# Moving four weight conversions of a dense MLP into the mixture-of-experts stage, and issuing a gather one expert earlier

## The chip, the cores and the metric

The kernel runs on one core of a Trainium2 chip. The metric is the device time of one execution in microseconds (us); the median of several runs is given. The core has TensorE (PE, matmuls; PEld is its loading of weights), VectorE (DVE), ScalarE (ACT), GpSimd (POOL) and SyncE (SP), which issues most of the transfers between the chip's main memory and the core's memory. Each engine works through its own list of instructions in order and waits on semaphores for the others.

## The reference, cut to what matters

Three blocks follow one another. Each takes the result of the one before.

```python
def _moe_ref(x, w_gate, w1, w2):              # x: the attention's output, 2304 tokens x 512
    logits = x @ w_gate
    expert_idx = np.argmax(logits, axis=1)
    ...
    for e in range(E):                        # 8 experts
        mask = expert_idx == e
        xe = x[mask]
        h = np.maximum(xe @ w1[e], 0.0)       # 512 -> 1024
        ye = h @ w2[e]                        # 1024 -> 512
        out[mask] = gate_w[mask, None] * ye
    return out.astype(np.float32)

def _moe2_ref(x, w_in, w_out):                # w_in and w_out are float64
    h = x @ w_in                              # 512 -> 2048
    g = np.where(pos, h, np.where(neg, 0.0, (h + beta) ** 2 / (4.0 * beta)))
    return (g @ w_out).astype(np.float32)     # 2048 -> 512
```

Ahead of them stands an attention with random features, which the change does not touch.

## The kernel before, in words

The attention is laid out by a planner (class Plan). From there on the order of every engine's instructions is the order in which the program is written.

Every product is made of three matmuls: each operand is split into a high part (rounded for the matmul) and a low part (the rest), and high x high, high x low and low x high are summed. So a weight chunk needs, after its load into a raw tile (wraw, three buffers), a high part wh on POOL (L270) and a low part wl. For w1 and w2 the low part is a subtraction on DVE (L279), which is put off to the next w_flush; for w_in and w_out it is a subtraction on POOL (L274). w_in and w_out are float64: before the split, each chunk of 128 x 512 numbers is turned into float32 by one ACT instruction (wx, L263) and three DVE instructions (wy L264, wy L265, wz L268).

The list wseq names all chunks in the order of their use: per expert four of w1 and four of w2, then per quarter of the dense MLP four of w_in and four of w_out. w_advance (L298) does one chunk: it flushes the low part of the chunk before, issues loads on SP up to two chunks beyond this one (w_fetch, ahead = 3) and starts the split. A load waits until the raw buffer that it takes over has been read, which for w1 and w2 means until the low part of the chunk three places before is done on DVE.

An expert e in the loop at L1097: eight hidden slices f = 0 to 7 (m_h): 12 matmuls (L984 to L986) into one of three PSUM buffers ph, then hh on ACT (L989) and hl on DVE (L990). After every even f one advance is made (a w2 chunk of this expert), after every odd f a flush. Then four output slices d = 0 to 3 (m_y, 24 matmuls each, L1002 to L1004, with yT copied out by ACT at L1007). Ahead of each, the tokens of the next expert are transposed (m_x, L946) and split into xh on ACT (L952) and xl on DVE (L953); the low part of the chunk before is flushed; after each one advance is made (a w1 chunk of the next expert). In experts 1 to 5 order_tokens adds three small DVE instructions (sob, sov) after odd f; in expert 5 it ends with a small store, ld (L1031), of 2304 single numbers to main memory.

The tokens of an expert are fetched by gather (L937): up to three indirect DMAs that POOL issues (L940), at the start of the expert before. At the start of the last expert stands overflow (L1037), a block of code behind a branch that is not taken with these inputs.

In the last expert the advances do its four w2 chunks, the first four chunks of w_in and three of w_out; z_split (L913) splits the columns of yT for the dense MLP into yh on ACT and yl on DVE (L919). The dense MLP (z_h, L1131) starts right behind.

## Time and profile before

| | |
|---|---|
| time, median of 3 runs | 843.32 us (840.59, 844.49, 843.32) |
| the profiled execution | 839.76 us, its span 838.0 us |
| mean granted clock of TensorE | 0.974 |
| PE busy | 783.4 us, 93% |
| PEld, DVE busy | 85%, 68% |
| ACT, POOL busy | 43%, 46% |

The span runs from the first to the last instruction. The attention ends near 170 us; the experts follow, each about 25 to 38 us long; the dense MLP's first matmuls stand near 420 us and the last matmul near 824 us. A busy share is an average over all these stages. Matmuls overlap, so that a matmul's own time is longer than the distance from one start to the next; a gap of PE is read from the idle time ahead of an instruction. The granted clock has two levels here, 1.0 (2.4 GHz) and 0.5 (1.2 GHz).

### The profile page before, as it was taken

Reading aid. Unit: us, or ns where it says so; the run is one execution under the profiler, and the core shown is the slowest. Engines: PE = TensorE matmul, PEld = TensorE weight load, DVE = VectorE, ACT = ScalarE, POOL = GpSimd, SP = SyncE. Lnnn points to the kernel's source line nnn. Section 1 sums busy time; section 2 is a strip of 40 time slices with the busy share of each in tenths; the row PEclk is TensorE's granted clock in tenths of the full one; section 3 lists DMA queues with packets and bytes.
Section 4 is the critical chain, followed back from the end, with each engine's and each line's share of the span. In section 5 each row is a group of like instructions: output and inputs, shape, how many; then the busy total and the mean of one; then the engine's idle time right before and its main releaser. Section 6 shows DMA issues by size and latency. Waiting matters only on the chain.

```text
span 838.0 us, 16906 instructions
## 1 busy us (share of the span) xinstructions
PE 783.4 (93%) x6530; PEld 714.3 (85%) x6530; DVE 573.9 (68%) x1122; ACT 357.7 (43%) x890; POOL 384.1 (46%) x387
## 2 busy tenths in 40 slices
PE   6898899689999999988899999999999999999994
PEld 5787788569999999988888989898989898989893
DVE  4789797955775576354988566686777877656631
ACT  6998799412222222211444554444343434343321
POOL 5547851544455434342565444454434543334343
PEclk9999899869999999999999999999999999999998
DMA  9876301255555545653522001110111100001111
GB/s 222 209 172 185 97 29 28 78 156 163 189 178 179 177 157 158 153 159 124 183 84 92 26 26 49 53 51 25 40 37 51 51 25 1 1 26 51 39 50 64
DMA packets 79036, 80.44 MB, mean 96 GB/s; under 512 B 28972, under 2 KB 61868, under 8 KB 78944
## 3 DMA queue, kind: packets, MB, share of 16 engines
q1 hardware_dynamic: 75056, 68.10, 28.4%
q0 software_dynamic: 3072, 9.57, 3.3%
q10 hardware_dynamic: 816, 1.57, 0.6%
q8 instruction: 54, 0.88, 0.4%
q14 instruction: 38, 0.31, 0.1%
HBM read 69.78 MB, written 9.45 MB: 95 GB/s over the span
## 4 chain that ended last, share of the span: by engine, by line
PE 48%; DVE 3%; DMA 2%; issue 1%; POOL 1%; ACT 0%; POOLq 0%; another core or an unknown queue 0%; DVEq 0%
PE po L1186 8%; PE po L1185 8%; PE po L1184 8%; PE ph L1140 8%; PE ph L1142 8%; PE ph L1141 8%; DVE wy L265 1%; DVE yl L919 1%; DMA out_dram<-acc,oidx 1%; DMA wraw<-in_moe_w_in_dram 1%; DMA wraw<-in_moe_w_dram 1%; DVE wy L264 0%; POOL gl L1169 0%; DVE wl L279 0%; PE ph L984 0%
## 5 line engine op out<-in xcount | busy, mean ns | idle before, releaser
L1169 POOL TENSOR_TENSOR gl<-cl,gh 128x384 fp32r<-128x384 f32 x96 | 104.6, 1110 | 167.5 <-ACT gh L1168 167.4
L1161 ACT ACTIVATE cl<-cl,half 128x384 f32<-128x384 f32 x96 | 57.0, 615 | 215.1 <-DVE cl L1160 215.1
L1141 PE MATMUL ph<-yl,wh 128*128 128x384 f32 x384 | 129.9, 338 | 1.8 <-DVE yl L919 1.8
L1140 PE MATMUL ph<-yh,wh 128*128 128x384 f32 x384 | 129.9, 338 | 0.0
L1142 PE MATMUL ph<-yh,wl 128*128 128x384 f32 x384 | 129.8, 338 | 0.0
L270 POOL TENSOR_SCALAR wh<-wraw 128x1024 fp32r<-128x1024 f32 x60 | 69.5, 1159 | 124.6 <-DMA wraw<-in_moe_w_dram 74.5
L1186 PE MATMUL po<-wh,gl 128*128 128x512 f32 x288 | 114.3, 397 | 0.1
L1185 PE MATMUL po<-wl,gh 128*128 128x512 f32 x288 | 113.8, 395 | 0.0
L1184 PE MATMUL po<-wh,gh 128*128 128x512 f32 x288 | 113.7, 395 | 0.0
L1160 DVE TENSOR_SCALAR cl<-ph 128x384 f32<-128x384 f32 x96 | 51.3, 550 | 77.8 <-PE ph L1142 77.0
L482 ACT ACTIVATE pp<-ps,bi 128x128 f32<-128x128 f32 x288 | 84.2, 476 | 6.1 <-DVE bi L478 6.1
L919 DVE TENSOR_TENSOR yl<-yT,yh 128x384 fp32r<-128x384 f32 x96 | 83.5, 927 | 4.3 <-ACT yh L918 4.3
L984 PE MATMUL ph<-xh,wh 128*128 128x288 f32 (+6 forms) x256 | 80.5, 314 | 5.8 <-DVE hl L990 3.2
L279 DVE TENSOR_TENSOR wl<-wraw,wh 128x1024 fp32r<-128x1024 f32 x60 | 75.0, 1251 | 12.1 <-POOL wh L270 12.1
L1002 PE MATMUL py<-hh,wh 128*128 128x288 f32 (+6 forms) x256 | 79.3, 310 | 1.8 <-ACT yT L1007 1.8
L985 PE MATMUL ph<-xl,wh 128*128 128x288 f32 (+6 forms) x256 | 78.8, 308 | 0.0
L986 PE MATMUL ph<-xh,wl 128*128 128x288 f32 (+6 forms) x256 | 78.6, 307 | 0.0
L1004 PE MATMUL py<-hh,wl 128*128 128x288 f32 (+6 forms) x256 | 76.8, 300 | 0.3 <-DVE wl L279 0.3
L1003 PE MATMUL py<-hl,wh 128*128 128x288 f32 (+6 forms) x256 | 76.5, 299 | 0.6 <-DVE hl L990 0.6
L1141 PEld LDWEIGHTS ph<-yl,wh 128*128 128x128 f32 x384 | 72.2, 188 | 4.1 <-DVE yl L919 2.2
L1140 PEld LDWEIGHTS ph<-yh,wh 128*128 128x128 f32 x384 | 72.2, 188 | 2.1
L1142 PEld LDWEIGHTS ph<-yh,wl 128*128 128x128 f32 x384 | 72.2, 188 | 0.0
(158 smaller groups left out, 1657.4 us busy)
## 6 DMA issues: line engine op xcount, KB each, us to landing
wraw<-in_moe_w_dram SPq DMA_DIRECT2D x57, 512.0 KB, 3.7
wraw<-in_moe_w_in_dram SPq DMA_DIRECT2D x16, 512.0 KB, 3.8
wraw<-in_moe_w_out_dram SPq DMA_DIRECT2D x16, 512.0 KB, 3.4
blk<-in_k_dram SPq DMA_DIRECT2D x8, 512.0 KB, 6.9
blk<-in_q_dram SPq DMA_DIRECT2D x8, 512.0 KB, 6.1
vm<-in_v_dram SPq DMA_DIRECT2D x16, 256.0 KB, 5.7
xd<-xr SPq DMA_DIRECT2D x16, 256.0 KB, 2.0
wra<-in_moe_w_dram SPq DMA_DIRECT2D x4, 512.0 KB, 7.1
```

What stands on the lines that cost most here:

```text
L482: act.activation(at(ppb)[:, 2 * j + i, :], at(pjb[i])[:, j, :], AF.Exp, bias=r["bi"][:, i, j:j + 1])
L919: nc.vector.tensor_sub(yl, yT[d][:, c], yh.bitcast(F32))
L984: nc.tensor.matmul(ph, lhsT=wh[:, d, c], rhs=xh, start=(d == 0), stop=False)
L985: nc.tensor.matmul(ph, lhsT=wh[:, d, c], rhs=xl, start=False, stop=False)
L1002: nc.tensor.matmul(py, lhsT=wh[:, a, c], rhs=hh, start=(f == 0), stop=False)
L1140: nc.tensor.matmul(ph[f], lhsT=wh[:, a, c], rhs=yh, start=(d == 0), stop=False)
L1141: nc.tensor.matmul(ph[f], lhsT=wh[:, a, c], rhs=yl, start=False, stop=False)
L1142: nc.tensor.matmul(ph[f], lhsT=wl[:, a, c], rhs=yh, start=False, stop=(d == 3))
L1169: nc.gpsimd.tensor_sub(gl, cl, gh.bitcast(F32))
L1184: nc.tensor.matmul(po, lhsT=gh[:, c], rhs=wh[:, a, :], start=(f == 0), stop=False)
L1185: nc.tensor.matmul(po, lhsT=gh[:, c], rhs=wl[:, a, :], start=False, stop=False)
L1186: nc.tensor.matmul(po, lhsT=gl[:, c], rhs=wh[:, a, :], start=False, stop=(f == 3))
```

## The change

A new kind of entry in wseq, ("early", chunk), stands behind the w2 chunks of experts 3, 4, 5 and 6, one for each of the four first w_in chunks. Its advance loads the float64 chunk and converts it (w_float32) into a float32 tile of its own, ws, of which there are four. Where the chunk has its old place in the last expert, nothing is loaded or converted any more; the high and low parts are taken from ws. The early advance is made at f = 6, straight behind that slice's own advance. The gather is issued in three parts after d = 1, 2 and 3, and for the expert after the next; expert 0 still issues the whole gather for expert 1 at its start.

```diff
     def w_load(key, t=None, dma=nc.sync):
-        kind, e, c = key
+        kind, e, c = key[1] if key[0] == "early" else key
...
+    def w_float32(t, out):
+
+        tv = t.rearrange("p (f two) -> p f two", two=2)
+        lv = tv[:, :, 0].bitcast(I32)
+        hv = tv[:, :, 1]
+        x = wp2[0].tile([P, 512], F32, name="wx", tag="wx", bufs=1)
+        y = wp2[0].tile([P, 512], I32, name="wy", tag="wy", bufs=1)
+        nc.scalar.activation(x, hv, AF.Copy, scale=2.0 ** -112)
+        nc.vector.tensor_scalar(out=y, in0=lv, scalar1=29, scalar2=None, op0=ALU.logical_shift_right)
+        nc.vector.scalar_tensor_tensor(out=y, in0=x.bitcast(I32), scalar=3, in1=y,
+                                       op0=ALU.logical_shift_left, op1=ALU.bitwise_or)
+        nc.vector.scalar_tensor_tensor(out=out.bitcast(I32), in0=hv.bitcast(I32), scalar=-2 ** 31, in1=y,
+                                       op0=ALU.bitwise_and, op1=ALU.bitwise_or)
...
     def w_split(key):
-        t = wraw.pop(key)
+        if key[0] == "early":
+
+            early = wearly[key[1]] = wst[0].tile([P, 512], F32, name="ws", tag="ws", bufs=4)
+            w_float32(wraw.pop(key), early)
+            return
+        t = wearly[key] if key in wearly else wraw.pop(key)
...
+            if key not in wearly:
+                raw, t = t, wp2[0].tile([P, 512], F32, name="wz", tag="wz", bufs=2)
+                w_float32(raw, t)
...
+    EARLY = {3 + c: ("wi", 0, c) for c in range(4)}
     for e in range(E):
         wseq += [("w1", e, c) for c in range(4)] + [("w2", e, c) for c in range(4)]
+        if e in EARLY:
+            wseq.append(("early", EARLY[e]))
...
         while wpos[0] < min(ahead[1], wpos[1] + ahead[0]):
-            w_load(wseq[wpos[0]], dma=dma)
+            if wseq[wpos[0]] not in EARLY.values():
+                w_load(wseq[wpos[0]], dma=dma)
             wpos[0] += 1
...
-        def gather(e):
-            t = mp.tile([P, NB, D], F32, name="xg", tag="xg", bufs=2)
+        def gather(e, parts=range(NB)):
+            if e >= E:
+                return
+            if 0 in parts:
+                xg[e] = mp.tile([P, NB, D], F32, name="xg", tag="xg", bufs=2)
             for i, r in rows(e):
-                nc.gpsimd.indirect_dma_start(
-                    out=t[0:r, i, :], out_offset=None, in_=xd,
-                    in_offset=bass.IndirectOffsetOnAxis(ap=gidx[0:r, i, e:e + 1], axis=0))
-            xg[e] = t
+                if i in parts:
+                    nc.gpsimd.indirect_dma_start(
+                        out=xg[e][0:r, i, :], out_offset=None, in_=xd,
+                        in_offset=bass.IndirectOffsetOnAxis(ap=gidx[0:r, i, e:e + 1], axis=0))
...
-            else:
-                gather(e + 1)
+            elif e == 0:
+                gather(1)
...
+                if f == 6 and e in EARLY:
+                    w_advance()
...
                     w_advance()
+
+                    if d:
+                        gather(e + 2, (d - 1,))
```

What this does to the lists of instructions is shown at three places, of the kernel before and then of the changed one. A row gives the line, the operation, what it writes and reads, and the shape. The line numbers of the changed kernel are others: L246, L247 and L249 are the three conversion instructions there, L288 is wl, L1010 hl, L973 xl, L279 wh, L961 the gather.

DVE in expert 4, from slice f = 5 to the first xl of expert 5, before:

```order
L279 TENSOR_TENSOR wl_3157<-wraw,wh_3156 128x1024
L990 SCALAR_TENSOR_TENSOR hl<-ph,hh 128x288 x2
L1014 TENSOR_SCALAR sob<-cs,spos 128x128
L1018 TENSOR_SCALAR sov<-cs,spos 128x18 x2
L279 TENSOR_TENSOR wl_3159<-wraw,wh_3158 128x1024
L953 TENSOR_TENSOR xl<-px,xh 128x304 x2
```

The same place of the changed kernel:

```order
L288 TENSOR_TENSOR wl_3157<-wraw,wh_3156 128x1024
L1010 SCALAR_TENSOR_TENSOR hl<-ph,hh 128x288
L288 TENSOR_TENSOR wl_3159<-wraw,wh_3158 128x1024
L246 TENSOR_SCALAR wy<-wraw 128x512
L247 SCALAR_TENSOR_TENSOR wy<-wx,wy 128x512
L249 SCALAR_TENSOR_TENSOR ws<-wraw,wy 128x512
L1010 SCALAR_TENSOR_TENSOR hl<-ph,hh 128x288
L1034 TENSOR_SCALAR sob<-cs,spos 128x128
L1038 TENSOR_SCALAR sov<-cs,spos 128x18 x2
L973 TENSOR_TENSOR xl<-px,xh 128x304 x2
```

The low part of the last w2 chunk now stands ahead of the last hl, and the three conversion instructions stand between the two.

POOL from the middle of expert 5's output slices to expert 6 (wh_84 to wh_90 are the w1 chunks of expert 6, wh_3152 and wh_3154 its first w2 chunks), before:

```order
L270 TENSOR_SCALAR wh_86<-wraw 128x1024
L270 TENSOR_SCALAR wh_88<-wraw 128x1024
L270 TENSOR_SCALAR wh_90<-wraw 128x1024
L940 DMA xg<-xd,gidx 128x512 x2
L940 DMA xg<-xd,gidx 88x512
L270 TENSOR_SCALAR wh_3152<-wraw 128x1024
L270 TENSOR_SCALAR wh_3154<-wraw 128x1024
```

POOL there in the changed kernel:

```order
L279 TENSOR_SCALAR wh_86<-wraw 128x1024
L961 DMA xg<-xd,gidx 128x512
L279 TENSOR_SCALAR wh_88<-wraw 128x1024
L961 DMA xg<-xd,gidx 128x512
L279 TENSOR_SCALAR wh_90<-wraw 128x1024
L961 DMA xg<-xd,gidx 88x512
L279 TENSOR_SCALAR wh_3152<-wraw 128x1024
L279 TENSOR_SCALAR wh_3154<-wraw 128x1024
```

The three gathers for expert 7 now stand behind the second, third and fourth w1 copy instead of together behind the fourth. On SP, the load of the float64 chunk of expert 5 now stands ahead of the store ld, where the load of the first w1 chunk of expert 6 stood, and all four w1 loads of expert 6 come behind ld instead of three.

DVE in the last expert, from slice f = 4 on, before:

```order
L279 TENSOR_TENSOR wl_3159<-wraw,wh_3158 128x1024
L264 TENSOR_SCALAR wy<-wraw 128x512
L265 SCALAR_TENSOR_TENSOR wy<-wx,wy 128x512
L268 SCALAR_TENSOR_TENSOR wz<-wraw,wy 128x512
L990 SCALAR_TENSOR_TENSOR hl<-ph,hh 128x344
L264 TENSOR_SCALAR wy<-wraw 128x512
L265 SCALAR_TENSOR_TENSOR wy<-wx,wy 128x512
L268 SCALAR_TENSOR_TENSOR wz<-wraw,wy 128x512
L990 SCALAR_TENSOR_TENSOR hl<-ph,hh 128x344 x2
L264 TENSOR_SCALAR wy<-wraw 128x512
L265 SCALAR_TENSOR_TENSOR wy<-wx,wy 128x512
L268 SCALAR_TENSOR_TENSOR wz<-wraw,wy 128x512
```

The same place of the changed kernel:

```order
L288 TENSOR_TENSOR wl_3159<-wraw,wh_3158 128x1024
L1010 SCALAR_TENSOR_TENSOR hl<-ph,hh 128x344 x3
L935 TENSOR_TENSOR yl<-yT_3169,yh 128x384
L246 TENSOR_SCALAR wy<-wraw 128x512
L247 SCALAR_TENSOR_TENSOR wy<-wx,wy 128x512
L249 SCALAR_TENSOR_TENSOR wz<-wraw,wy 128x512
L246 TENSOR_SCALAR wy<-wraw 128x512
L247 SCALAR_TENSOR_TENSOR wy<-wx,wy 128x512
L249 SCALAR_TENSOR_TENSOR wz<-wraw,wy 128x512
L935 TENSOR_TENSOR yl<-yT_3170,yh 128x384
```

Four groups of three conversion instructions are gone from between and behind the last hl; those that are left belong to w_out.

## Rows read from the trace of the kernel before

**Rows 1.** Timeline, PE: start us, us, what, [idle before it <-releaser].
```profile
360.04 0.42 PE L984 MATMUL ph<-xh,wh 128*128 128x328 f32 x1 [3.17 <-DVE hl L990]
...
385.25 0.63 PE L984 MATMUL ph<-xh,wh 128*128 128x344 f32 x1 [2.31 <-POOL wh L270]
...
405.68 0.43 PE L1003 MATMUL py<-hl,wh 128*128 128x344 f32 x1 [0.61 <-DVE hl L990]
...
416.07 0.43 PE L1002 MATMUL py<-hh,wh 128*128 128x344 f32 x1 [1.82 <-ACT yT L1007]
...
423.19 0.45 PE L1141 MATMUL ph<-yl,wh 128*128 128x384 f32 x1 [1.84 <-DVE yl L919]
```

**Rows 2.** Windows: from:to, length, busy (count) PE, PEld, DVE, ACT, POOL, clock, DMA.
```profile
361.24:364.65 3.41, 3.41 (x14) 3.41 (x13) 2.14 (x4) 0.44 (x1) 1.05 (x1) 0.50 0.76 249
364.65:368.10 3.45, 3.45 (x25) 3.44 (x25) 1.68 (x3) 1.24 (x3) 1.05 (x1) 1.00 0.49 144
...
410.00:420.00 10.00, 8.18 (x53) 7.90 (x52) 9.45 (x11) 3.76 (x7) 6.82 (x7) 1.00 0.46 157
```

**Rows 3.** Line L1043, the branch of overflow: ns min/median/max, first and last start.
```profile
L1043 PEldq COMPARE_BRANCH  x1: 4093/4093/4093, 380.7 to 380.7; - x1
```

**Rows 4.** Groups by line, DVE, 399 to 436 us: busy us, mean ns.
```profile
L265 DVE SCALAR_TENSOR_TENSOR wy<-wx,wy 128x512 int32<-128x512 int32 x9 | 10.3, 1140 | 2.4 <-ACT wx L263 1.6
```

**Rows 5.** Timeline, DVE, last expert.
```profile
399.75 0.42 DVE L264 TENSOR_SCALAR wy<-wraw 128x512 int32<-128x512 int32 x1
400.28 0.69 DVE L265 SCALAR_TENSOR_TENSOR wy<-wx,wy 128x512 int32<-128x512 int32 x1
...
401.61 0.51 DVE L990 SCALAR_TENSOR_TENSOR hl<-ph,hh 128x344 fp32r<-128x344 f32 x1
...
402.88 1.59 DVE L265 SCALAR_TENSOR_TENSOR wy<-wx,wy 128x512 int32<-128x512 int32 x1
```

**Rows 6.** Timeline, DVE: hl of slices 6 and 7, experts 3 and 5.
```profile
275.93 0.86 DVE L990 SCALAR_TENSOR_TENSOR hl<-ph,hh 128x280 fp32r<-128x280 f32 x2
...
331.98 0.47 DVE L990 SCALAR_TENSOR_TENSOR hl<-ph,hh 128x304 fp32r<-128x304 f32 x1
```

**Rows 7.** Timeline, DVE: the low part that waited longest, expert 6.
```profile
347.38 1.22 DVE L279 TENSOR_TENSOR wl<-wraw,wh 128x1024 fp32r<-128x1024 f32 x1 [5.47 <-POOL wh L270]
```

**Rows 8.** Timeline, PE: users of hl 7 (experts 3, 5), of wl and xl (expert 6).
```profile
279.37 0.29 PE L1003 MATMUL py<-hl,wh 128*128 128x280 f32 x1
...
336.42 0.30 PE L1003 MATMUL py<-hl,wh 128*128 128x304 f32 x1
...
348.00 0.31 PE L986 MATMUL ph<-xh,wl 128*128 128x328 f32 x1
...
349.21 0.31 PE L985 MATMUL ph<-xl,wh 128*128 128x328 f32 x1
```

**Rows 9.** Timeline, POOL: first two w1 copies for expert 4.
```profile
276.31 1.04 POOL L270 TENSOR_SCALAR wh<-wraw 128x1024 fp32r<-128x1024 f32 x1 [1.91 <-PE px L946]
279.65 1.04 POOL L270 TENSOR_SCALAR wh<-wraw 128x1024 fp32r<-128x1024 f32 x1 [2.30 <-DMA wraw<-in_moe_w_dram]
```

**Rows 10.** Timeline, POOL, last expert.
```profile
402.58 1.34 POOL L274 TENSOR_TENSOR wl<-wz,wh 128x512 fp32r<-128x512 f32 x1
```

**Rows 11.** DMA issues, 320 to 400 us: count, KB each, us to landing.
```profile
ld<-slf SPq DMA_DIRECT2D x1, 9.0 KB, 14.6
```

**Rows 12.** Timeline, POOL, end of expert 5 and start of expert 6.
```profile
346.31 1.05 POOL L270 TENSOR_SCALAR wh<-wraw 128x1024 fp32r<-128x1024 f32 x1 [11.91 <-PE py L1004]
348.48 1.05 POOL L270 TENSOR_SCALAR wh<-wraw 128x1024 fp32r<-128x1024 f32 x1 [1.13 <-DMA wraw<-in_moe_w_dram]
...
351.85 2.00 POOL L940 DMA_INDIRECT xg<-xd,gidx  x1 [0.16 <-issue]
354.16 0.95 POOL L940 DMA_INDIRECT xg<-xd,gidx  x1 [0.30 <-issue]
...
356.43 2.07 POOL L270 TENSOR_SCALAR wh<-wraw 128x1024 fp32r<-128x1024 f32 x2
```

More of the change, by code (lines that the diff above doesn't have):

```diff
@@ L257, in w_split @@
             lo = lo[:, (c % 2) * 512:(c % 2) * 512 + 512]
-            tv = t.rearrange("p (f two) -> p f two", two=2)
-            lv = tv[:, :, 0].bitcast(I32)
-            hv = tv[:, :, 1]
-            x = wp2[0].tile([P, 512], F32, name="wx", tag="wx", bufs=1)
-            y = wp2[0].tile([P, 512], I32, name="wy", tag="wy", bufs=1)
-            nc.scalar.activation(x, hv, AF.Copy, scale=2.0 ** -112)
-            nc.vector.tensor_scalar(out=y, in0=lv, scalar1=29, scalar2=None, op0=ALU.logical_shift_right)
-            nc.vector.scalar_tensor_tensor(out=y, in0=x.bitcast(I32), scalar=3, in1=y,
-                                           op0=ALU.logical_shift_left, op1=ALU.bitwise_or)
-            t = wp2[0].tile([P, 512], F32, name="wz", tag="wz", bufs=2)
-            nc.vector.scalar_tensor_tensor(out=t.bitcast(I32), in0=hv.bitcast(I32), scalar=-2 ** 31, in1=y,
-                                           op0=ALU.bitwise_and, op1=ALU.bitwise_or)
+            if key not in wearly:
+                raw, t = t, wp2[0].tile([P, 512], F32, name="wz", tag="wz", bufs=2)
+                w_float32(raw, t)
         nc.gpsimd.tensor_scalar(out=hi, in0=t, scalar1=1.0, scalar2=1.0, op0=ALU.mult, op1=ALU.mult)
@@ L285 @@
     wseq = []
+    wearly = {}
+    wst = []
+    EARLY = {3 + c: ("wi", 0, c) for c in range(4)}
     for e in range(E):
         wseq += [("w1", e, c) for c in range(4)] + [("w2", e, c) for c in range(4)]
+        if e in EARLY:
+            wseq.append(("early", EARLY[e]))
     for qd in range(4):
@@ L924 @@
         mps = mctx
+        wst.append(mp)
         ps_x = mps.enter_context(tc.tile_pool(name="ps_x", bufs=2, space=PSUM))
```

## The prediction

> **What bounds the kernel now.** I went down to one stretch and stayed there. First, the timeline of TensorE. From 180 us to the last matmul it runs almost without a break: apart from gaps under half a microsecond there are five, and [rows 1] show the matmul behind each. Their idle times are 3.17, 2.31, 0.61, 1.82 and 1.84 us. The reader is to see the clock time and the releaser of each. The first stands in expert 6, the second before the first matmul of expert 7, the third in the second half of expert 7, the fourth before its last output slice, the fifth in the first matmuls of the dense MLP. Second, the windows of the granted clock, because a gap can cost more than its length: the 3.41 us behind the first gap ran at 0.50, which is 1.2 of 2.4 GHz, with 14 matmuls started, and the next 3.45 us at 1.00 with 25 [rows 2]. Fourteen matmuls at that second pace take 1.9 us, so the first gap cost another 1.5 us. The three gaps of 405 to 423 us were not followed by a lower clock; the window around the fourth of the five has 1.00 [rows 2]. Third, the timelines of the engines that PE waited for.
>
> **The branch is out of the sum.** The 2.31 us gap at 385.25 is put down to POOL, but TensorE's own branch over the overflow code took 4.09 us there [rows 3]. The change keeps that branch and leaves PE's order of instructions as it was, so I carry this gap at zero change.
>
> **Last expert and start of the MLP: what goes.** Four chunks of w_in were converted there on VectorE, three instructions each: L264, L265, L268. Undisturbed, the three take from 399.75 to the hl behind them at 401.61, 1.86 us with hand-overs; a disturbed L265 took 1.59 instead of 0.69 us [rows 5], and over the stretch from 399 us its mean was 1.14 [rows 4]. With L268 like it and L264 at 0.42, a chunk costs 1.9 to 2.7 us, and these four hold VectorE for 7.4 to 10.8 us, in front of the hl and yl that end the last three gaps. They leave. What is late next? The two copies of hl 6 and 7 then follow h 6 and 7 directly. Three chunks of w_out stay, behind yl of output slices 0, 0 and 1. They and the three later yl cost 3 x 2.7 + 3 x 0.5 = 9.6 us at most, while PE is busy with three more slices of 24 matmuls, 9.9 us at the pace of 25 in 3.45 us [rows 2]. The yl of the last slice comes three instructions of about half a microsecond each (taken like the hl of [rows 5]) after the last output matmul, and 18 MLP matmuls, 2.5 us, stand ahead of its use. So I take all three gaps out: 0.61 + 1.82 + 1.84 = 4.3 us. Bounds: nothing to lose here, since no instruction is added to this stretch; at least 2.4 us if yl stays late once as in the last gap. GpSimd's hi and lo halves of the four chunks stay there, and run earlier than before, since they no longer wait for VectorE.
>
> **Experts 3 to 6: what is added.** In each, at the seventh hidden slice (f = 6), a second advance stands on VectorE between hl 6 and hl 7: the lo half of the last w2 chunk (moved up from behind hl 7), then the three conversion instructions. Queued behind them are hl 7, the ordering instructions and the xl of the next expert; TensorE waits for hl 7 in the last but one matmul of the first output slice. Worked out for expert 3: hl 6 ends at 275.93 + 0.43 = 276.36 [rows 6]; the lo half 1.22 [rows 7] makes 277.58; conversion 1.86 makes 279.44; hl 7 another 0.43, 279.87. PE reaches its matmul at 279.37 [rows 8]. Late by 0.5 us. The raw chunk is in time: its load takes the place that the first w1 chunk of the next expert had, and GpSimd's copy of that chunk began at 276.31 [rows 9], 1.3 us before VectorE gets to the conversion; the ScalarE step fits into that. Expert 4 repeats this, 0.5 us. Expert 5: 331.98 + 0.47 [rows 6] + 1.22 + 1.86 + 0.47 = 336.0, and PE comes at 336.42 [rows 8], so nothing. Expert 6 starts late for another reason (below) and has room; nothing. Sum 1.0 us. From below it could be nothing (the lo half came after hl 7 before; its move up costs no time), from above 2.7 us per expert more, where all three instructions are blocked like the L265 of 1.59 us. I take the undisturbed value because GpSimd's next copy, whose chunk is now loaded one place later, can be expected where the one after it stood before, at 279.65 [rows 9], when the conversion has ended.
>
> A rule that speaks against the change: L265 took 0.69 us with GpSimd idle and 1.59 us when started at 402.88, beside GpSimd's subtraction of 402.58 to 403.92 [rows 5, 10]; it ended 0.55 us behind it. The Trainium skill (SBUF — State Buffer, section "SBUF: two separate sides") says that VectorE and GpSimd share a port pair under an exclusive lock, and that an instruction with two SBUF inputs, as these are, waits out a GpSimd instruction that reads SBUF. By that rule the trace agrees, and with a copy of GpSimd always in the way the sum would be that of the slower rival below.
>
> **Start of expert 6: a wait that moves, and one that goes.** In expert 5 the DMA of ld took 14.6 us to land [rows 11], and the weight load issued behind it was awaited by GpSimd for 11.91 us, until 346.31 [rows 12]. Before, that was the second w1 chunk of expert 6; now an extra load stands ahead of ld, so the first w1 chunk is the one behind ld, and all four are. I take the same landing times. Then the lo half of chunk 0 runs on VectorE at 347.38 to 348.60 [rows 7], and PE's third matmul of expert 6 needs it, at 348.00 before [rows 8]: 0.6 us late. Behind it comes xl of slice 2, then the lo half of chunk 1 (its hi half starts at 348.48 [rows 12] and takes 1.05, so the lo half ends at 350.8), then xl of slice 3 (half a microsecond, like the hl of [rows 5]) at 351.3. PE's eleventh matmul wants that at 349.21 [rows 8] + 0.6 = 349.8: 1.4 us late. New: 2.0 us, in two pieces, none as long as the gap behind which the clock fell.
>
> Against that, the first gap of [rows 1]. There the three gathers held GpSimd from 351.85 to 356.4, and the copy of the first w2 chunk began only at 356.43 [rows 12]; its lo half, then hl 2, then PE's slice 5, which needs the PSUM buffer. Now the gathers for expert 7 stand one by one between the w1 copies of expert 5's second half. From 349.5, three gathers of 0.95 + 0.3 us, two w1 copies and the w2 copy of 1.05 each make about 356.5; lo half and hl 2 end near 358.2. PE gets to slice 5 at 360.04 - 3.17 + 2.0 = 358.9. So the gap goes, with 0.7 us to spare, and the 1.5 us of half clock with it. Stage: 2.0 - 3.2 - 1.5 = -2.7 us. Bounds: -4.7 (nothing new late) to +1.2 (gathers of 2.00 us as at 351.85; the second rival).
>
> Elsewhere the gathers go from the start of an expert into the second half of the one before; experts 1 to 5 show no gap at either place, so nothing.
>
> **Sum.** 1.0 - 2.7 - 4.3 = -6.0 us. The profiled execution took 839.76 us around a span of 838.0; that becomes 833.8. It lay 3.6 us under the median of 843.32, so against the median I expect 843.3 - 6.0 = 837.3 us.
>
> **Rivals.**
> Gathers slowed. A gather beside a VectorE subtraction took 2.00 us, the next one 0.95 [rows 12]; now all three stand among such subtractions. Three times 1.05 more puts hl 2 at 361.3, 2.4 us late; the clock falls as before. Stage 2.0 + 2.4 - 3.2 = +1.2, in all 1.0 + 1.2 - 4.3 = -2.1: 841.2 us. For it: that one row; against it: the two others of the same three.
> Nothing new is late. If ld's neighbours land earlier and the conversion fits, -3.2 - 1.5 - 4.3 = -9.0: 834.3 us. For it: PE waits for the last but one matmul only, and half a microsecond is close.
> The MLP keeps a gap. The w_out conversions meet GpSimd's halves, yl stays 2 us late: -4.0, 839.3 us.
> The lock, which ends slower: GpSimd's copies fall into each conversion, each of the three instructions loses 0.9 us, hl 7 is 3.2 us late in experts 3 and 4, 2.3 in 5 and 2.0 in 6, and each gap is followed by 1.5 us of half clock as in [rows 2]: 10.7 + 6.0 - 2.7 - 4.3 = +9.7, 853.0 us. It decides from about 2.8 us lost per expert on. Against it: the GpSimd rows have one copy per 3 us there, not one per instruction [rows 9].
>
> **How the numbers follow.** My forecast 0.45, with 834.5 to 839.5 as its own range; gathers slowed 0.25; nothing late 0.15; MLP gap 0.07; lock 0.08. A measurement of this kernel tells about 0.5% (4.2 us) from no change, so faster means under 839.1. Faster: 0.40 of the forecast, 0.15, and 0.07 from the edges of the second and fourth: 0.62. Same: 0.30. Slower: 0.08. Range 832.5 to 842.5: below, "nothing late" with some of the scatter of the three runs; above, "gathers slowed" with the same; left out are mainly the lock and the far ends.
>
> **What would show it.** Right: no idle of PE over 0.3 us between 400 and 425; hl-released waits of about 0.5 us near the end of the first output slice of experts 3 and 4; two waits of together 2 us in the first dozen matmuls of expert 6, and no clock of 0.50 in expert 6. The gap of the branch still there at about 2.3 us. Wrong: PE idle over 2 us at hl 7 in any of experts 3 to 6, conversion instructions of 1.5 us there, gathers of 2 us, or a half-clock stretch in expert 6.

## The result and the profile after

The changed kernel takes 832.54 us, the median of 6 runs (831.91 to 835.8), the kernel before 842.85 in 6 runs beside it (838.52 to 845.02). The ratio is 0.9895, with a 95% interval of 0.9867 to 0.9923: 10.3 us faster, where 6.0 were forecast. A second comparison gave 0.9929 (0.9898 to 0.9960), 12 runs against 17. The two intervals have 0.9898 to 0.9923 in common, a gain of 6.5 to 8.6 us.

The changed kernel was also profiled twice. The table reads each stage from the first matmul of an expert, or of the MLP, to that of the next, the MLP's to the start of the last matmul (827.0 us before the change, not near 824, and 823.0 us after it); the sums are taken from the ends and can differ by 0.1 us of rounding. The attention and expert 0 are left out, since their end moved by several microseconds from profile to profile of kernels that have the same code there (the first matmul of expert 0 came between 177.2 and 181.4 us).

| stage, us | before | forecast | after | after, again |
|---|---|---|---|---|
| experts 1 and 2 | 53.7 | 0 | 53.7 | 53.2 |
| expert 3 | 27.9 | +0.5 | 28.0 | 27.9 |
| expert 4 | 28.4 | +0.5 | 28.9 | 28.4 |
| expert 5 | 28.6 | 0 | 32.7 | 31.2 |
| expert 6 | 37.5 | -2.7 | 34.0 | 35.0 |
| expert 7 | 34.7 | with the MLP | 31.8 | 30.2 |
| dense MLP | 407.1 | -4.3 for both | 404.3 | 405.0 |
| sum | 617.9 | -6.0 | 613.3 (-4.6) | 610.9 (-7.0) |

So the forecast of the sum lies between the two profiles, but its terms do not stand where it put them. Expert 5 lost what it was not to lose, and the last expert and the MLP won more than they were to win. Experts 5 and 6 together were to win 2.7 us and lost 0.6 and 0.1, so the whole gain stands in the last expert and the MLP.

Where PE waited behind the attention in the changed kernel's first profile, in the four places of over half a microsecond and in one shorter one that the prediction had named (start us, us, what; in brackets the idle time before it and its releaser):

```profile
308.56 0.40 PE L1023 MATMUL py<-hl,wh 128*128 128x288 f32 x1 [0.25 <-DVE hl L1010]
...
338.66 0.40 PE L1022 MATMUL py<-hh,wh 128*128 128x304 f32 x1 [1.05 <-ACT hh L1009]
340.19 0.62 PE L1023 MATMUL py<-hl,wh 128*128 128x304 f32 x1 [1.12 <-DVE hl L1010]
...
363.41 0.42 PE L1004 MATMUL ph<-xh,wh 128*128 128x328 f32 x1 [1.23 <-DVE hl L1010]
...
386.98 0.40 PE L1004 MATMUL ph<-xh,wh 128*128 128x344 f32 x1 [2.07 <-PEq L1063]
```

The four long ones stand against the five of [rows 1]. The yl and yT waits of the last expert and the MLP are gone, and so is the 3.17 us for hl in expert 6; 1.2 of it is left. The wait of the branch (L1063) is still there. New are the rows of L1022 and L1023. The first row, of 0.25 us, is the end of the first output slice of expert 4. The next two are the same place of expert 5: hh and hl of hidden slice 7, which the forecast had in time by 0.4 us [rows 6, 8]. The windows of the same kernel (columns as in [rows 2]; the last two are the busy share of the DMA engines and the GB/s that they moved), around the place in expert 5 and over the last expert and the MLP's start:

```profile
339.90:343.35 3.45, 3.16 (x13) 3.13 (x14) 1.14 (x3) 0.87 (x2) 0.00 (x0) 0.51 0.65 28
343.40:346.80 3.40, 3.40 (x27) 3.40 (x26) 0.00 (x0) 0.76 (x2) 0.00 (x0) 1.00 0.86 162
...
397.00:421.00 24.00, 24.00 (x153) 24.00 (x152) 15.61 (x20) 8.67 (x18) 17.04 (x16) 1.00 0.42 135
420.00:432.00 12.00, 12.00 (x64) 11.18 (x63) 9.81 (x18) 7.10 (x14) 6.38 (x7) 1.00 0.25 84
```

Expert 5 now has the half clock that stood behind the first gap of expert 6: 13 matmuls in 3.45 us, then 27 in 3.40. In the last two windows PE is busy for 24.00 of 24.00 and 12.00 of 12.00 us: the third, fourth and fifth gaps of [rows 1] are closed.

Why hh and hl 7 were late: DVE in expert 5.

```profile
333.54 1.22 DVE L288 TENSOR_TENSOR wl<-wraw,wh 128x1024 fp32r<-128x1024 f32 x1
337.56 0.43 DVE L246 TENSOR_SCALAR wy<-wraw 128x512 int32<-128x512 int32 x1 [2.80 <-DMA wraw<-in_moe_w_in_dram]
338.33 0.69 DVE L247 SCALAR_TENSOR_TENSOR wy<-wx,wy 128x512 int32<-128x512 int32 x1 [0.34 <-ACT wx L245]
339.06 0.69 DVE L249 SCALAR_TENSOR_TENSOR ws<-wraw,wy 128x512 int32<-128x512 int32 x1
339.67 0.47 DVE L1010 SCALAR_TENSOR_TENSOR hl<-ph,hh 128x304 fp32r<-128x304 f32 x1
```

The conversion's own instructions take 0.43, 0.69 and 0.69 us, undisturbed. But the first waits 2.80 us for the load of the float64 chunk, and hl 7 stands behind all three. On ACT the conversion's wx waits for the same load, ahead of hh 7, which L1022 waits for:

```profile
337.62 0.68 ACT L245 ACTIVATE wx<-wraw 128x512 f32<-128x512 f32 x1 [4.50 <-DMA wraw<-in_moe_w_in_dram]
338.19 0.42 ACT L1009 ACTIVATE hh<-ph 128x304 fp32r<-128x304 f32 x1
```

SP issued that load here:

```profile
330.69 0.35 SPq L232 DMA_DIRECT2D wraw<-in_moe_w_in_dram  x1
331.99 0.39 SPq L1051 DMA_DIRECT2D ld<-slf  x1
```

The load goes out 1.30 us ahead of ld, and is seen as landed only 6.87 us after its issue (337.56 - 330.69). Over 320 to 400 us the median landing of the loads of w1 and w2 (in_moe_w_dram) is 3.8 us, and ld takes about as long as in [rows 11] (the DMA view, columns as there):

```profile
ld<-slf SPq DMA_DIRECT2D x1, 9.0 KB, 14.3
wraw<-in_moe_w_dram SPq DMA_DIRECT2D x18, 512.0 KB, 3.8
```

POOL, end of expert 5 and expert 6, answers to [rows 12]:

```profile
347.88 1.05 POOL L279 TENSOR_SCALAR wh<-wraw 128x1024 fp32r<-128x1024 f32 x1 [16.31 <-DMA wraw<-in_moe_w_dram]
...
351.25 2.00 POOL L961 DMA_INDIRECT xg<-xd,gidx  x1 [0.16 <-issue]
...
354.51 1.97 POOL L961 DMA_INDIRECT xg<-xd,gidx  x1 [0.17 <-issue]
...
357.78 1.98 POOL L961 DMA_INDIRECT xg<-xd,gidx  x1 [0.20 <-issue]
359.79 2.07 POOL L279 TENSOR_SCALAR wh<-wraw 128x1024 fp32r<-128x1024 f32 x2
```

All four w1 chunks are behind ld, as forecast, and POOL now idles for 16.31 us. The high part of chunk 0 is begun at 347.88, and PE begins expert 6 only at 353.02, so nothing is late there. All three gathers take 2 us, as the rival "gathers slowed" had it, and the first w2 copy starts at 359.79, later than before (356.43, [rows 12]).

### The profile page after: what moved, and what is told of

It is laid out like the page before. It is cut to its first block, busy times and chain, and to the rows that moved or that the text cites. A ratio compares the mean times of both kernels' runs of the same rounds, so it can differ in the third digit from the quotient of the medians.

```text
span 834.0 us, 16899 instructions
## 1 busy us (share of the span) xinstructions
PE 779.9 (94%) x6530; PEld 711.4 (85%) x6530; DVE 567.9 (68%) x1122; ACT 358.5 (43%) x890; POOL 394.1 (47%) x387
## 3 DMA queue, kind: packets, MB, share of 16 engines
q1 hardware_dynamic: 75056, 68.10, 28.9%
## 4 chain that ended last, share of the span: by engine, by line
PE 52%; DMA 1%; issue 0%; POOLq 0%; DVE 0%
PE ph L1165 8%; PE ph L1166 8%; PE ph L1167 8%; PE po L1211 8%; PE po L1210 8%; PE po L1209 8%; PE ph L1004 1%; PE ph L1006 1%; PE ph L1005 1%; DMA out_dram<-acc,oidx 1%; PE py L1024 1%; PE py L1022 1%; PE py L1023 1%; POOLq L1267 0%; DVE acc L1217 0%
## 5 line engine op out<-in xcount | busy, mean ns | idle before, releaser
L279 POOL TENSOR_SCALAR wh<-wraw 128x1024 fp32r<-128x1024 f32 x60 | 74.3, 1240 | 114.1 <-DMA wraw<-in_moe_w_dram 63.5
L288 DVE TENSOR_TENSOR wl<-wraw,wh 128x1024 fp32r<-128x1024 f32 x60 | 77.4, 1291 | 14.4 <-POOL wh L279 14.4
L935 DVE TENSOR_TENSOR yl<-yT,yh 128x384 fp32r<-128x384 f32 x96 | 80.7, 898 | 9.3 <-ACT yh L934 9.3
L1004 PE MATMUL ph<-xh,wh 128*128 128x288 f32 (+6 forms) x256 | 78.7, 308 | 3.7 <-PEq L1063 2.1
L1022 PE MATMUL py<-hh,wh 128*128 128x288 f32 (+6 forms) x256 | 79.7, 311 | 1.1 <-ACT hh L1009 1.1
L1023 PE MATMUL py<-hl,wh 128*128 128x288 f32 (+6 forms) x256 | 77.3, 302 | 1.4 <-DVE hl L1010 1.4
L1005 PE MATMUL ph<-xl,wh 128*128 128x288 f32 (+6 forms) x256 | 77.1, 301 | 0.1
```

Source lines behind the costliest of these rows:

```text
L1004: nc.tensor.matmul(ph, lhsT=wh[:, d, c], rhs=xh, start=(d == 0), stop=False)
L1005: nc.tensor.matmul(ph, lhsT=wh[:, d, c], rhs=xl, start=False, stop=False)
L1022: nc.tensor.matmul(py, lhsT=wh[:, a, c], rhs=hh, start=(f == 0), stop=False)
L1023: nc.tensor.matmul(py, lhsT=wh[:, a, c], rhs=hl, start=False, stop=False)
```

## The experiments

After the profile two things had to be told apart: which part of the change the gain belongs to, the conversions' leaving the last expert or the gather's new place; and whether the stall of expert 5 comes from the conversion's own work or from the store ld, whose damage then only moved from expert 6 to expert 5. The second table has the stages of every run, read as above. "Half" names the experts in which 3.41 us of half clock was granted.

| kernel | ratio to before (95%) | expert 5 | expert 6 | 7 and MLP | half | from expert 1 |
|---|---|---|---|---|---|---|
| before | 1 | 28.6 | 37.5 | 441.8 | 6, 7 | 617.9 |
| after | 0.9895 (0.9867, 0.9923) | 32.7 | 34.0 | 436.1 | 5, 7 | 613.3 |
| after, again | 0.9929 (0.9898, 0.9960) | 31.2 | 35.0 | 435.2 | none | 610.9 |
| conv_only | 0.9962 (0.9929, 0.9995) | 32.9 | 36.3 | 435.3 | 5, 6 | 614.6 |
| gather_only | 0.9993 (0.9961, 1.0026) | 28.6 | 37.1 | 442.1 | 6, 7 | 617.9 |
| before_no_ld | 0.9949 (0.9921, 0.9977) | 28.6 | 32.0 | 441.8 | none | 612.0 |
| after_no_ld | 0.9896 (0.9854, 0.9937) | 28.6 | 32.4 | 436.1 | 7 | 606.7 |
| early_1to4 | 0.9919 (0.9886, 0.9951) | 28.6 | 34.6 | 435.0 | none | 609.3 |
| ld_rows | 0.9881 (0.9849, 0.9914) | 28.8 | 32.1 | 435.5 | none | 606.4 |
| ld_rows_conv | 0.9854 (0.9817, 0.9890) | 28.8 | 32.2 | 436.2 | 7 | 607.6 |

**The conversions alone, the gather as before** (conv_only).

```diff
-        def gather(e, parts=range(NB)):      # in parts, for e + 2
+        def gather(e):                       # whole, for e + 1
...
-            elif e == 0:
-                gather(1)
+            else:
+                gather(e + 1)
...
-                    if d:
-                        gather(e + 2, (d - 1,))
```

> The changed kernel with the gather put back: whole, at the start of the expert before. Theory: the conversions moved out of the last expert are worth some 7 us (the three gaps of 405 to 423 us and their wake), while the gathers at the start of expert 6 again hold GpSimd up behind the late loads, so that this version keeps only part of the gain: 836 to 840 us against 842.9 before, with a gap of over 2 us in expert 6. Rival 'the gather does nothing': within 1 us of the changed kernel's 832.5, no gap of over 2 us in expert 6.

Measured: 836.94 us, against 840.2 for the kernel before on the same chip. The last expert and the MLP take 435.3 us as in the changed kernel: that gain belongs to the conversions alone. The stall in expert 5 is there too (32.9 us), so it is not the gather's. PE's waits from 300 to 440 us:

```profile
PE ph L1001 <- DVE hl L1007: 2.3, 1, 2.3
...
PE py L1020 <- DVE hl L1007: 1.3, 2, 1.1
PE py L1019 <- ACT hh L1006: 1.1, 1, 1.1
```

The first row is the gap of expert 6, over 2 us as the theory had it, with the half clock behind it. It is shorter than 3.17 us: PE begins expert 6 3.2 us later than before (350.92 against 347.71), POOL its first w2 copy only 2.4 us later (358.80 against 356.43). The interval overlaps that of the second comparison of the changed kernel (0.9898 to 0.9960), so that by the times alone the gather's new place is not told from nothing.

**The gather alone** (gather_only): the reverse edit of the one above, on the kernel before.

> The kernel before with only the gather issued ahead in three parts. Theory: the gap of 3.17 us in expert 6 and the half clock behind it go or shrink, the three gaps of 405 to 423 us stay: 3 to 5 us faster than before, 838 to 840 us. Rival 'the gather does nothing': 842 to 844 us, with the 3 us gap in expert 6 still there. Rival 'the gather is the whole gain': 832 to 834 us.

Measured: 838.61 us, a ratio that reaches from 0.9961 to 1.0026: no difference that can be told, at most 3.3 us. The theory wanted 3 to 5, and the stages of the profile sum to 617.9 us as before; the rival 'the gather does nothing' holds. (The microseconds of both were written for a kernel before of 842.9 us; on this chip it took 840.2.) The gap of expert 6 stayed, in two pieces; PE's waits and POOL's gathers:

```profile
PE ph L987 <- DVE hl L993: 2.6, 2, 2.0
```

```profile
348.25 2.00 POOL L944 DMA_INDIRECT xg<-xd,gidx  x1 [0.16 <-issue]
...
354.78 1.98 POOL L944 DMA_INDIRECT xg<-xd,gidx  x1 [0.20 <-issue]
356.78 2.08 POOL L270 TENSOR_SCALAR wh<-wraw 128x1024 fp32r<-128x1024 f32 x2
```

The gathers begin 3.6 us earlier than in [rows 12], but all three take 2 us (the second 1.97) where it was one of three, and they alternate with the copies of late chunks. The first w2 copy starts at 356.78, where it was 356.43. Nothing came forward.

**The store left out, in both kernels** (before_no_ld, after_no_ld).

```diff
-                nc.sync.dma_start(out=ld.rearrange("(t p) o -> p t o", p=P), in_=lf)
```

> The kernel before without the store ld (see above). Theory: the wait of GpSimd of 11.9 us, the gap of 3.17 us in expert 6 and its half clock go: 4 to 5 us less than before, near 838 us. Rival 'the gathers alone make that gap': it stays, 842 to 844 us.

> The changed kernel without the store ld (2304 single numbers to main memory, read only by the overflow code, which does not run with these inputs). Theory: this store delays the load of the float64 chunk in expert 5 and the w1 loads behind it, so without it the gaps of expert 5 near hl 7, the half clock behind them and the gap of expert 6 all go: 4 to 6 us less than the changed kernel, 827 to 829 us. Rival 'VectorE itself is late in expert 5': the gaps of expert 5 stay, 831.5 to 833 us.

Measured: 835.0 and 830.23 us, on a chip where the kernel before took 840.2 and the changed kernel did not run. The first is 5.2 us less than before, a little more than the theory's 4 to 5. The second lies above the 827 to 829 expected, and its ratio of 0.9896 is that of the changed kernel's first comparison (0.9895); against the second (0.9929) it is 2.8 us less. So what the store costs the changed kernel is not shown by these times. The profile shows it: 606.7 us from expert 1 on, against 613.3 and 610.9. Without the store the kernel before takes 32.0 us for expert 6 in place of 37.5, and the old gather is in time. POOL there:

```profile
343.68 1.04 POOL L940 DMA_INDIRECT xg<-xd,gidx  x1 [0.16 <-issue]
345.02 0.95 POOL L940 DMA_INDIRECT xg<-xd,gidx  x1 [0.30 <-issue]
346.27 0.98 POOL L940 DMA_INDIRECT xg<-xd,gidx  x1 [0.30 <-DMA wraw<-in_moe_w_dram]
```

They start 8.2 us earlier than the 351.85 of [rows 12], on the same lines of the program. So the first gap of [rows 1] was the store's work: it held up a w1 chunk, that held up POOL, and POOL's gathers and w2 copy came late. In the changed kernel without the store both stalls are gone, and PE waits for one thing from 300 to 440 us:

```profile
PE ph L1004 <- POOL wh L279: 2.2, 1, 2.2
```

That one is the matmul behind the branch. What the store did to all traffic of the core is read from the windows behind it, of the changed kernel and of the changed kernel without ld:

```profile
335.50:343.00 7.50, 5.32 (x28) 4.83 (x27) 3.10 (x6) 2.19 (x5) 0.00 (x0) 0.80 0.55 28
```

```profile
333.00:341.00 8.00, 8.00 (x61) 8.00 (x60) 4.42 (x8) 2.33 (x7) 3.76 (x4) 1.00 0.75 246
```

In the first window two weight loads, issued at 333.12 and 334.88, were on their way all the time and a third from 339.87 on, and 28 GB/s were moved; in the second it was 246.

Between the two kernels without the store the difference is 5.3 us from expert 1 on (612.0 and 606.7; 4.8 us by the medians): what the change is worth when ld disturbs neither. Expert 6, where the gather's new place was to help, takes 32.0 and 32.4 us, so that it is the conversions' move that is worth it.

**The changed kernel again** (after_again, no edit).

> The changed kernel once more, unaltered, beside the kernel before on one chip. Theory (the gain is what the stages of the two profiles show, 4 us from the span and 6.4 from the start of expert 0 on): ratio 0.992 to 0.996; in the profile expert 5 takes 32.8 us and expert 6 34.0 again within 0.5, the first matmul of expert 0 somewhere from 178 to 182 us. Rival (the first comparison's 0.9895 is the change's own, and something outside these stages is faster): ratio 0.987 to 0.991 again.

Measured: 834.95 us against 840.71. Theory and rival met in the middle: 0.9929 is inside the theory's range, and its interval contains the rival's upper end. The profile had 31.2 and 35.0 us for experts 5 and 6 where 32.8 and 34.0 were expected within 0.5, and its first matmul of expert 0 came at 177.7 us, just ahead of the 178 to 182 expected. The waits in expert 5 are the same (1.0 for hh, 1.1 for hl), but no half clock followed. The window behind them:

```profile
336.70:340.20 3.50, 3.46 (x25) 3.46 (x26) 0.89 (x2) 0.76 (x2) 0.00 (x0) 1.00 0.64 25
```

25 matmuls in 3.50 us, against 13 in 3.45 at 0.51 behind the same two waits.

**The conversions beside experts 1 to 4** (early_1to4).

```diff
-    EARLY = {3 + c: ("wi", 0, c) for c in range(4)}
+    EARLY = {1 + c: ("wi", 0, c) for c in range(4)}
```

> The changed kernel with the four conversions beside experts 1 to 4. Theory (the 4 us that expert 5 lost are the float64 load issued 1.3 us ahead of the ld store and landing with it): expert 5 takes 28.4 us in place of 32.8, with no PE idle over 0.5 us at 335 to 342; PE then comes 4 us earlier to expert 6 and waits there as the kernel with the new gather alone did (step of 2.3 us, half clock, 37.1 in place of 34.0), so that the time is within 1 to 2 us of the changed kernel: span 832 to 834, ratio 0.991 to 0.995. Rival (the four conversion instructions fill DVE and make hl 7 late wherever the fourth of them stands): expert 4 takes 32 to 33 us, expert 5 28.5, expert 6 34 to 37.

Measured: 834.08 us, a ratio of 0.9919. Expert 5 takes 28.6 us and PE waits for nothing there, and expert 4, which now has the fourth conversion, takes 28.6 as well: four conversions on DVE are not enough for the stall, and the rival is out; what expert 5 lost was the float64 load beside ld. The gap of expert 6 came back at 2.0 us, as the theory had it; the half clock behind it did not, so that expert 6 took 34.6 us and not 37.1. PE's waits from 300 to 440 us:

```profile
PE ph L1004 <- PEq L1063: 2.0, 1, 2.0
PE ph L1004 <- DVE hl L1010: 2.0, 1, 2.0
```

Against the changed kernel on the same chip it is 0.9 us, which cannot be told. Experts 5 and 6 take 3.0 us less than in that kernel's second profile, but experts 1 and 2 take 54.6 us where it was 53.2. There hl 7 is late by 0.61 and 0.45 us: the wait that the prediction had for experts 3 and 4, two experts earlier.

One row speaks against too simple a rule. The load that takes the place ahead of ld here is one of w1, issued 1.27 us ahead (333.76 and 335.03), and by the DMA view it lands after 3.5 us; so does the one 1.11 us ahead in the kernel before. In gather_only a w1 load 1.95 us ahead took 8.9 us. The float64 load was late in all three executions that have it there: 6.87 us (as seen by DVE), 6.6 and 6.8 (after again and conv_only). Without the store it takes 3.8. Why the one kind was held and the other not always stays open.

**ld stored as rows** (ld_rows). The same 9 KB, on the same queue, one step later.

```diff
+            if t == NTILE + 1:
+                nc.tensor.transpose(pq[0:NTILE, P:2 * P], ldt[0][:, :, 0], ident)
+                lr = mp.tile([NTILE, P], F32, name="slr", tag="slr", bufs=1)
+                nc.vector.tensor_copy(lr, pq[0:NTILE, P:2 * P])
+                nc.sync.dma_start(out=ld.rearrange("(t p) o -> t (p o)", p=P), in_=lr)
...
-                nc.sync.dma_start(out=ld.rearrange("(t p) o -> p t o", p=P), in_=lf)
+                ldt.append(lf)
```

> The changed kernel with ld turned on PE (one transpose of 128x18) and stored as 18 rows of 512 bytes in place of 2304 single elements of 4 bytes; the same 9 KB, on the same queue, one step later. Theory (the store's many small pieces hold up the loads around it): ld lands in 2 to 4 us instead of 14.3, expert 5 takes 28.4 to 28.9 us, expert 6 28.6 to 29.0, and the span is 826 to 828: as with the store left out (826.1), ratio 0.987 to 0.991 and some 5 to 7 us under the changed kernel on this chip. Rival (any store at this place holds them, or it is the transfers' own order): expert 5 takes 32 to 33 us and the ratio is that of the changed kernel.

Measured: 830.03 us, 4.9 us under the changed kernel on the same chip, a little less than the 5 to 7 expected, and 10.7 under the kernel before. The span of 824.2 lies below the expected 826 to 828. Expert 5 takes 28.8 us, inside the theory's range. The ratio is inside the 0.987 to 0.991. The 28.6 to 29.0 us that this expectation and the next give for expert 6 were misread (it is expert 5's stage); expert 6 takes 32.1 us here, and 32.0 and 32.4 in the two kernels with the store left out. DVE in expert 5 has no wait for the load, and SP sends the row store between the weight loads:

```profile
331.31 0.42 DVE L246 TENSOR_SCALAR wy<-wraw 128x512 int32<-128x512 int32 x1
331.98 0.69 DVE L247 SCALAR_TENSOR_TENSOR wy<-wx,wy 128x512 int32<-128x512 int32 x1 [0.25 <-ACT wx L245]
...
333.32 0.47 DVE L1010 SCALAR_TENSOR_TENSOR hl<-ph,hh 128x304 fp32r<-128x304 f32 x1
```

```profile
327.40 0.35 SPq L232 DMA_DIRECT2D wraw<-in_moe_w_in_dram  x1
...
334.00 0.38 SPq L1051 DMA_DIRECT2D ld<-slr  x1
334.63 3.07 SPq L227 DMA_DIRECT2D wraw<-in_moe_w_dram  x2
```

PE waits for one thing, the branch; POOL has its first w1 chunk of expert 6 at 334.08 us, where the changed kernel got it at 347.88:

```profile
PE ph L1004 <- PEq L1070: 1.9, 1, 1.9
```

For the loads behind the store this settles it. The one issued 0.63 us behind the row store lands after 4.0 us, the one issued 1.13 us behind ld in the changed kernel after 14.6 (the DMA view of that one issue), and 204 GB/s are moved from 334 to 342 us: neither the bytes nor the queue held them, but the 2304 single elements of 4 bytes. For the float64 load ahead of it this run shows nothing, since the load landed at 331.18 us, 2.8 us before the row store went out; there after_no_ld alone has the proof. The DMA view gives no landing time for the row store; the trace's packets have 18 of 512 bytes between 334.80 and 336.23 us, inside the 2 to 4 us expected.

**Rows for ld and the gather as before** (ld_rows_conv): the two edits together.

> The kernel with the ld rows, but the gather as it was before (whole, for the next expert). Theory (the gather was late at expert 6 only because the store held up what POOL waited for, so that the gather's new place has nothing left to win): expert 6 takes 28.6 to 29 us without a PE wait over 0.5 us, and the time is within 1 us of the ld rows with the new gather. Rival (the old gather is late by itself): a PE wait of 2 to 3 us in the first third of expert 6 and 1.7 us at half clock behind it, 3.5 to 4.5 us slower than ld rows with the new gather.

Measured: 827.99 us, a ratio of 0.9854 (0.9817 to 0.9890), beside 0.9881 (0.9849 to 0.9914) for the rows with the new gather: no difference that can be told. The medians are 2.0 us apart, more than the theory's 1 us, and in favour of the old gather. The rival's 3.5 to 4.5 us do not appear, and PE waits for nothing in expert 6. The old gathers are quick in their old place:

```profile
345.14 1.04 POOL L957 DMA_INDIRECT xg<-xd,gidx  x1 [0.15 <-issue]
...
347.85 0.98 POOL L957 DMA_INDIRECT xg<-xd,gidx  x1 [0.31 <-issue]
```

Expert 6 takes 32.2 us with them. This version and ld_rows beat both kernels on the chip on which all four ran. Between the two, the simpler one, without the gather's move, does as well.

## Why the prediction came out as it did

**Direction and sum.** Faster was right. 832.54 us lies 0.04 us above the lower end of the range, and that it lies inside is luck: the reason given for that end was that nothing new would be late, and something was. The forecast's -6.0 us sits between -4.6 and -7.0 of the two profiles. Measured by medians it was -10.3 the first time and -5.8 the second (834.95 and 840.71), so part of the first is the scatter of the runs that were compared. That the sum fits is luck too, since errors of both signs met: experts 5 and 6, -2.7 forecast, gave +0.6 and +0.1, and the last expert with the MLP, -4.3 forecast, gave -5.7 and -6.6. Of the signs that the prediction named, no idle of PE from 400 to 425 us, full clock in expert 6 and the gap of the branch came; but so did two of those that were to show it wrong, over 2 us of PE idle at hl 7 of expert 5, in two pieces, and gathers of 2 us.

**The step that failed: "Expert 5: ... and PE comes at 336.42, so nothing."** It lost 4.1 us in one profile and 2.6 in the other. The working added up DVE's instructions and took the raw chunk as in time, an argument made for expert 3 and carried over. In expert 5 the load goes out 1.30 us ahead of ld. The prediction had placed that load there ("an extra load stands ahead of ld") and followed only the loads behind. conv_only has the stall without the gather's move, early_1to4 loses it by moving the conversion and its load, and after_no_ld, where the conversion stays in expert 5, by leaving out the store: the cause is settled. What in the store held a load that was issued ahead of it is not. Hidden slice 7 came 2.2 us late in two waits, and 1.5 us more hung on the half clock, by which the two profiles differ (32.7 - 31.2 us).

**Start of expert 6, +2.0: did not appear.** All four w1 chunks came behind ld as forecast, but PE arrived 5.3 us later than before (353.02 against 347.7), 4.1 us of it by the stall of expert 5. The wait was covered rather than absent: without the stall PE would have come near 348.9 us (an estimate, 353.02 - 4.1), and the low part of chunk 0 ended at 350.19, that of chunk 1 at 352.36. In early_1to4, where expert 5 lost nothing, there was no wait there either: one w1 chunk fewer stands behind ld once the extra load is gone.

**The gap of expert 6, -3.2 and -1.5: half right.** The gap shrank and full clock came back in expert 6, but the rival "gathers slowed" had the mechanism: three gathers of 2 us. Its 2.4 us late came out as 1.2 in the first profile, since PE was late itself, and 2.0 in the second and in early_1to4; the half clock behind it appeared in gather_only and conv_only, but not in after, again or early_1to4. The forecast's cause was wrong further back. It read from [rows 12] that the gathers filled POOL, and moved them; before_no_ld shows that they stood there because a w1 chunk was held by ld [rows 11]. The row with 11.91 us of idle was the cause, and the rows of the gathers its effect.

**Experts 3 and 4, +0.5 each.** Expert 3 took 0.1 us more and nothing, expert 4 0.5 and nothing. The 0.5 is the forecast's own wait, at hl 7 (308.56 us above), and early_1to4 has it in experts 1 and 2; so the mechanism is right, but the wait is so short that it came in three of the eight places where these three traces have a conversion in an expert from 1 to 4. The conversion ran undisturbed (0.43, 0.69, 0.69 us), as the undisturbed value taken; the lock rival, which needs instructions of 1.5 us there, did not come. In the last expert, where three conversions stayed, it did. DVE and POOL of the changed kernel there:

```profile
413.01 1.67 DVE L249 SCALAR_TENSOR_TENSOR wz<-wraw,wy 128x512 int32<-128x512 int32 x1
...
416.01 1.59 DVE L247 SCALAR_TENSOR_TENSOR wy<-wx,wy 128x512 int32<-128x512 int32 x1
```

```profile
412.52 1.61 POOL L283 TENSOR_TENSOR wl<-wz,wh 128x512 fp32r<-128x512 f32 x1
...
415.71 1.34 POOL L283 TENSOR_TENSOR wl<-wz,wh 128x512 fp32r<-128x512 f32 x1
```

Both ended 0.55 us behind the end of POOL's subtraction (414.68 against 414.13, 417.60 against 417.05), as did the row in the prediction. The Trainium skill (SBUF — State Buffer, section "SBUF: two separate sides") says that a VectorE instruction with two SBUF inputs waits out a GpSimd instruction that reads SBUF and started first. The trace agrees with it in these rows. Beside experts 3 to 6 of this kernel no POOL instruction stood beside the conversion's last two instructions.

**Last expert and MLP, -4.3: mis-sized.** It measured -5.7 and -6.6 us. All three gaps closed, as forecast, but the first of them was larger than the profile of before showed. There the half clock behind the branch had already held PE up by 1.5 us, so that PE came later to a VectorE that was late in any case. before_no_ld has no half clock there, takes 34.8 us for expert 7 all the same, and has this first gap:

```profile
399.84 0.43 PE L1003 MATMUL py<-hl,wh 128*128 128x344 f32 x1 [2.08 <-DVE hl L990]
```

It is 2.08 us in place of the 0.61 of [rows 1]; the other two are 1.79 and 1.84, where [rows 1] have 1.82 and 1.84. Set matmul against matmul from the branch on, the changed kernel's second profile, without half clock too, gains on before_no_ld 2.5, 2.1 and 2.0 us at these three places, 6.6 in all, and nothing elsewhere. In the first profile the half clock came behind the branch, and now PE had no other engine to wait for: expert 7 took 31.8 us and not 30.2, the MLP 404.3 and not 405.0, together 0.9 us more. So the failed size is the 0.61 us: 2.5 was to be won there.

**The branch gap, unchanged.** Right: 2.07 us of idle, where it was 2.31. In the other kernels it lay between 1.7 and 2.2 us.

## What to carry to other kernels

A store of many single elements is read by its landing time: where a 9 KB transfer takes 14 us, ask of every load that goes out near it, ahead as well as behind, who waits for it; turn it into rows before moving work around its damage. A gap that is read behind a stretch of half clock is too small for what its engine is late by: where PE was slow just ahead, part of the lateness is hidden, and the slow stretch itself cost nothing. When a wait is found behind an instruction that came late, follow that engine's own idle time back one step more, since the instruction may be late for the same cause as all else there. Work that is put ahead of a needed result brings its load's lateness along, and that has to be checked at each place it repeats, not at one.

## What the runs showed of the hardware

The store of 2304 elements of 4 bytes held the loads behind it: 14.3 us to its own landing in the changed kernel and 15.7 in conv_only, 14.6 us to that of the load issued 1.13 us behind it, POOL idle for up to 16.56 us (conv_only), and 28 GB/s moved by the whole core from 335.5 to 343 us. As 18 rows of 512 bytes it held no load behind it: 4.0 us to the landing of the one 0.63 us behind, and 204 GB/s from 334 to 342 us. A float64 load issued 1.14 to 1.30 us ahead of it was late as well (6.6 to 6.9 us in place of 3.8, three executions); w1 loads 1.11 and 1.27 us ahead were not.

A gather is slow beside a low-part subtraction (wl) of VectorE that started first. Of the gathers behind 180 us in the ten traces, 75 began while one was running, and each ended 0.80 to 0.96 us behind its end; the 108 others took 0.86 to 1.04 us, 40 of them although a subtraction began meanwhile. So the second gather of before_no_ld, started at 345.02, took 0.95 us beside the first row below, and the first one for expert 7 in the changed kernel, started at 351.25, took 2.00 us beside the second row, 1.23 us long and started 0.12 us earlier:

```profile
345.07 1.22 DVE L279 TENSOR_TENSOR wl<-wraw,wh 128x1024 fp32r<-128x1024 f32 x1
```

```profile
351.13 1.23 DVE L288 TENSOR_TENSOR wl<-wraw,wh 128x1024 fp32r<-128x1024 f32 x1 [0.53 <-POOL wh L279]
```

The store has no part in it: in after_no_ld, without it, the second and third gather for expert 7 take 1.79 and 1.83 us. The new place invites it, since a gather stands there right behind a copy of POOL, and that copy is what VectorE was waiting for. The trace of before had such rows ahead of the change too (1.82, 1.55 and 1.80 us at 206.95, 233.64 and 260.86), where the prediction weighed one. No run was made for this alone.

The half clock is no fixed price of a wait. Behind two waits in expert 5, 1.05 and 1.12 us in one execution of the changed kernel and 0.97 and 1.12 in the other, the one was granted 0.51 for 3.45 us and the other 1.00; behind the branch gap it fell in five of the ten profiled executions here, at an idle time of 1.82 us (gather_only), and not at 2.05 (after, again). What it costs depends on who is late: with the moved conversions expert 7 took 31.8 us with it and 30.2 without in the changed kernel, and the MLP 404.3 and 405.0; with the conversions in their old place expert 7 and the MLP took 441.8 us with it (before) and 441.8 without (before_no_ld). What decides whether it comes stays open.
